# Who subtracts the low parts of the weights in a routed expert kernel: VectorE for GpSimd from the first tile on

## The chip, the cores and the metric

The kernel runs on one core of one Trainium2 chip. A core has five engines that go through their own instructions in order and wait for one another by semaphores: TensorE (PE in the profile) multiplies, VectorE (DVE) and ScalarE (ACT) work on elements, GpSimd (POOL) does so too and issues the DMAs that gather or scatter rows by a list of indices, and SyncE (SP) issues plain DMAs. The metric is the device time of one execution in microseconds; lower is better.

## The reference

A causal mixture over seven earlier positions (a softmax over 7 weights for each of 8 heads) gives 28672 tokens of 192 numbers. A router gives each token to one of 8 experts, by the sorted order of all logits and with room for 3584 tokens in each expert. Each token then goes through its expert's two layers.

```python
logits = x @ w_gate                       # x: 28672 x 192, w_gate: 192 x 8
flat = logits.flatten()
order = np.argsort(-flat)
...
for idx in order:
    tok, e = (int(idx) // E, int(idx) % E)
    if assigned[tok] >= 0 or counts[e] >= cap:
        continue
    assigned[tok] = e
    counts[e] += 1
...
for e in range(E):
    mask = assigned == e
    h = np.maximum(x[mask] @ w1[e], 0.0)  # w1[e]: 192 x 1024
    out[mask] = h @ w2[e]                 # w2[e]: 1024 x 192
```

## The kernel before

**Two stages.** First the mixture is made with Toeplitz matrices on TensorE (`cv`), transposed on VectorE (`aT`), and multiplied with the gate (`pl`, `bg`); the mixed rows go to `attn` in DRAM. This lasts to some 168 us. Then comes the expert stage: 56 tiles of 512 tokens, 7 of each expert. Tile i needs its tokens' rows (`xg`, four gathers by GpSimd, issued two tiles ahead), their transposes and both layers. The loop of `run` goes over tiles i and, within a tile, over eight steps f. A step makes an eighth of layer 1 of tile i (`l1`: five matmuls into a PSUM bank `ph`, of which there are three; ScalarE makes the rounded high part `hh`, VectorE the low part `hl`), a piece of the next tile's preparation (`prep`), half a block of layer 2 of tile i - 1 (`l2`: eight matmuls into `y`), every second step the sum of its halves on VectorE (`yo`) and a scatter to the output on GpSimd.

**High and low parts.** All matrices are split in a rounded high part and the low rest. `wsplit` does this for the weights, piece by piece: ScalarE rounds the raw piece to the high part, then an engine `eng` subtracts it from the raw piece, and SyncE stores both in DRAM for the later tiles of that expert and loads the next raw piece into the buffer that came free (`raw`, four buffers). An expert has eight pieces: `a`, `d`, `a`, `d` (layer 1, rows 0 to 127 and 128 to 191, two halves of the columns each; the low part of a `d` is `dl`) and four of `w` (layer 2). A step of `run` splits at most one piece. The first eight tiles are one of each expert. In tile i the four `w` of its own expert are split in the steps 0 to 3, and the four of layer 1 of the next expert in the steps 4 to 7. With the ninth tile on, weights come back from DRAM, already split. The tests in the last line that the change touches give `d` pieces to VectorE and the others to GpSimd.

**Routing beside the tiles.** Which token belongs to which expert is found out while tiles are running. Five generators make the lists: `half(0)` (512 tokens of each expert, there when the first tile begins), `tail` (the last gate products), `half(1)`, `rest` (rounds of a search for the thresholds, then a list) and `last`. A list is sorted with small matmuls against one-hot tiles that VectorE makes (`oa`). The generators' steps are put between the matmuls when the program is written: `Pace` keeps an account of when each engine will be done (`pe`, `dve`, `act`), and `hook` puts in the next step only while VectorE's account is less than 1.8 us ahead of TensorE's. `Meter` makes the entries, for instructions of TensorE, VectorE and ScalarE. GpSimd has no account: `nc.gpsimd` is the bare engine. Where a result is needed, `drain` runs its generator to the end at once: ahead of tile 1 (`tail`), and in `idx_of` ahead of the first gathers of a list (those of the tiles 8, 24 and 27, issued two tiles earlier).

**Two ways to transpose.** While generators are left, `prep` transposes a tile's rows on TensorE (`px`, one PSUM buffer, emptied by ScalarE and VectorE into `xa` and `xd`). Once they are done (`ff.free`, `free()`), VectorE does it with 16 transposes (`xs`).

Of the kernel before, what the change touches and what calls it, by code (L numbers as in the profile page):

```python
# [1336 lines left out]
def moe_kernel(ctx, tc, x, weight, wg, w1, w2, out):  # L1337
    nc = Pace(tc.nc)
    V, P = nc.vector, nc.gpsimd
# [4 lines left out]
    with ExitStack() as cw:  # L1344
# [11 lines left out]
        ff = FFN(tc, nc, attn, w1, w2, out, r.ident, wr, drm)  # L1356
# [21 lines left out]
        def half(h):  # L1378
            if h == 0:
                yield from r.thresh(0.905)  # L1380
            yield from r.settle(h)
            yield from r.count(r.F, h)
            if h:
                yield from r.counts(NE)
            yield from r.lists(r.F, TA, h, 0 if h else None, *((ia, ja) if h else (ia0, ja0, 8, 4)))

        def rest():
            yield from r.open()
            yield from r.rounds()
            yield from r.final(NL)  # L1390
            yield from r.lists(r.F, TB, 1, None, ib0, jb0, NL, 4)

        def last():
            yield from r.lists(r.F, TB, 0, 1, ib, jb)

        def tail():

            for i in (14, 15):
                for u in range(3):
                    gate(i, u)  # L1400
                    yield PEA if u == 2 else None
                end(i)
            nc.sync.dma_start(r.ltab, LT)
            c1.close()
            cs.close()
            ff.wpool2(cw, 1)
            ff.hp[1] = pool(cw, "fh1", 1, **late)
            yield

        bg = Steps(nc, r, (half(0), tail(), half(1), rest(), last()))  # L1410
# [121 lines left out]
            if i == 1:  # L1532
                bg.drain(3)

        VN = 64
        VP = (1, 3)
        ff.free = set()
        ff.run(idx_of, at, lambda f: P if bg.gens and (ff.done % 8 not in VP or ff.done >= VN) else V, lambda: not bg.gens)
    bi = lst.tile([128, 1], I32, name="bi")
    nc.vector.tensor_copy(bi, r.bad)  # L1540
    bad = nc.values_load(bi[0:1, 0:1], min_val=0, max_val=1)
# [31 lines left out]
```

## Time and profile before

| | |
|---|---|
| median of 3 runs | 1309.41 us (1309.36 to 1313.63) |
| the profiled execution | 1309.36 us, span 1307.3 us |
| TensorE busy | 95% of the span, granted clock 0.982 on average |
| VectorE, ScalarE, GpSimd busy | 77%, 42%, 43% |
| GpSimd's subtractions of weights | 50, of which 48 for `a` and `w` |
| expert stage | from some 168 us to the end |

The busy time of an engine is the time in which one of its instructions ran, waits for data left out. A line such as `L55 DVE ... out<-in xcount | busy, mean | idle before <-releaser` is a group of instructions: L55 is the line of the helper through which nearly all of them are written, so that groups are told apart by the names of their tiles. Numbers of buffers are left out: `X` stands for several scratch tiles of the routing.

### The profile page before, as it was taken

The numbers are of one execution on the slowest core, as the hardware profiler recorded it, in microseconds if no ns is written. First come the engines' busy times: TensorE is split into PE (matmuls) and PEld (weight loads), VectorE is DVE, ScalarE is ACT, GpSimd is POOL, SyncE is SP. The second block draws the span as 40 slices with busy tenths as digits, with TensorE's granted clock in tenths as the row PEclk, the third lists the DMA queues.
The fourth block names the chain that finished last, engine by engine and source line by source line (L and its number), as shares of the span: only waits on it lengthen the run. The fifth ranks groups of instructions, "written<-read, shape, count | busy, mean of one in ns | idle before, by whom it ended". The sixth has DMA issues, their size and how long they took to land.

```text
span 1307.3 us, 21815 instructions
## 1 busy us (share of the span) xinstructions
PE 1247.7 (95%) x7879; PEld 1072.5 (82%) x7879; DVE 1005.3 (77%) x2215; ACT 551.0 (42%) x1214; POOL 556.1 (43%) x549
## 2 busy tenths in 40 slices
PE   5789989988999999999999999999999999999997
PEld 3345568877888988888889999999999999999996
DVE  7488558789998998898757777777777777777772
ACT  5444544574534443443334333333333333333341
POOL 3000457567554344452334444444444444444422
PEclk9999988999999999999999999999999999999999
DMA  9999978579624343342222622332413232131100
GB/s 236 310 292 299 297 260 287 187 260 307 231 96 137 104 148 123 107 148 84 76 90 88 204 97 79 109 102 95 149 41 99 95 102 91 53 135 46 46 25 27
DMA packets 92931, 188.30 MB, mean 144 GB/s; under 512 B 12352, under 2 KB 57872, under 8 KB 88592
## 3 DMA queue, kind: packets, MB, share of 16 engines
q1 hardware_dynamic: 63888, 120.75, 29.4%
q0 software_dynamic: 21504, 44.07, 11.0%
q10 hardware_dynamic: 7424, 22.02, 4.5%
q8 instruction: 63, 1.03, 0.3%
q14 instruction: 52, 0.43, 0.1%
HBM read 114.44 MB, written 72.35 MB: 143 GB/s over the span
## 4 chain that ended last, share of the span: by engine, by line
PE 80%; DVE 9%; DMA 5%; issue 2%; SPq 1%; ACT 1%; POOL 1%; POOLq 0%; DVEq 0%; ACTq 0%
PE ph L55 36%; PE y L55 35%; PE bg L55 3%; DVE X L55 3%; PE cv L55 3%; DMA X<-in_x_dram 3%; DVE hl L55 2%; PE px L55 1%; PE pl L55 1%; DVE aT L55 1%; DMA wgr<-in_moe_w_gate_dram 1%; DMA attn<-a 1%; DMA raw<-in_moe_w_dram 1%; DVE oa L55 1%; SPq L187 0%
## 5 line engine op out<-in xcount | busy, mean ns | idle before, releaser
L55 PE MATMUL y<-w,hh 128*128 128x384 f32 x1792 | 543.0, 358 | 0.0
L55 ACT ACTIVATE hh<-ph 128x512 fp32r<-128x512 f32 x448 | 267.7, 598 | 496.6 <-PE ph L55 472.9
L55 PE MATMUL y<-w,hl 128*128 128x192 f32 x1792 | 450.9, 252 | 0.0
L55 DVE SCALAR_TENSOR_TENSOR hl<-ph,hh 128x512 fp32r<-128x512 f32 x448 | 307.8, 688 | 169.6 <-ACT hh L55 149.2
L55 PE MATMUL ph<-xa,w 128*128 128x512 f32 x1344 | 399.7, 405 | 3.9 <-DVE hl L55 3.9
L55 PEld LDWEIGHTS y<-w,hh 128*128 128x128 f32 x1792 | 339.1, 189 | 22.9 <-issue 6.1
L55 PEld LDWEIGHTS y<-w,hl 128*128 128x128 f32 x1792 | 343.4, 192 | 15.2
L1254 POOL DMA_INDIRECT out_dram<-yo,ib x128 | 128.4, 1003 | 287.7 <-DVE yo L55 277.5
L55 PEld LDWEIGHTS ph<-xa,w 128*128 128x128 f32 x1344 | 221.4, 191 | 24.2 <-DVE hl L55 4.7
L55 DVE STREAM_TRANSPOSE xs<-xg 32x256 f32<-32x256 f32 (+1 forms) x512 | 188.6, 368 | 8.8
L1254 POOL DMA_INDIRECT out_dram<-yo,ia x96 | 105.4, 1098 | 205.0 <-DVE yo L55 169.0
L55 PE MATMUL ph<-xd,w 128*128 128x512 f32 x448 | 179.2, 400 | 1.1 <-DVE xd L55 1.1
L55 PE MATMUL ph<-xd,dl 128*128 128x512 f32 x448 | 175.9, 393 | 1.9 <-DVE dl L55 1.6
L1179 POOL DMA_INDIRECT xg<-attn,jb x128 | 138.2, 1080 | 40.9 <-issue 40.9
L1179 POOL DMA_INDIRECT xg<-attn,ja x96 | 111.8, 1164 | 29.0 <-issue 26.7
L55 PE MATMUL cv<-X,TH 118*128 118x384 f32 x256 | 102.4, 526 | 21.6 <-DVE TH L55 12.5
L55 ACT ACTIVATE yt<-y 128x192 f32<-128x192 f32 x224 | 73.4, 328 | 113.1 <-PE y L55 102.7
L55 DVE TENSOR_TENSOR yo<-y,yt 128x192 f32<-128x192 f32 x224 | 79.5, 355 | 44.0 <-ACT yt L55 40.5
L55 PEld LDWEIGHTS ph<-xd,dl 128*128 128x128 f32 x448 | 85.1, 190 | 22.7 <-DVE dl L55 2.5
L55 PEld LDWEIGHTS ph<-xd,w 128*128 128x128 f32 x448 | 85.1, 190 | 21.2 <-DVE xd L55 1.6
L55 PEld LDWEIGHTS cv<-X,TH 118*128 118x128 f32 x256 | 45.3, 197 | 54.8 <-issue 20.4
L1160 POOL TENSOR_TENSOR w<-raw,w 128x384 fp32r<-128x384 f32 (+1 forms) x48 | 54.1, 1137 | 72.7 <-ACT w L55 37.8
(235 smaller groups left out, 985.7 us busy)
## 6 DMA issues: line engine op xcount, KB each, us to landing
w<-kw SPq DMA_DIRECT2D x16, 1536.0 KB
w<-kv SPq DMA_DIRECT2D x16, 1536.0 KB
X<-in_x_dram SPq DMA_DIRECT2D x16, 1344.0 KB
attn<-a ACTq DMA_DIRECT2D x16, 1344.0 KB
kw<-w SPq DMA_DIRECT2D x48, 256.0 KB
kv<-w SPq DMA_DIRECT2D x32, 384.0 KB
raw<-in_moe_w_dram SPq DMA_DIRECT2D x32, 192.0 KB
raw<-in_moe_w_dram SPq DMA_DIRECT2D x16, 256.0 KB
```

The source lines that it names most:

```text
L55: return f(*a, **k)
L1160: eng.tensor_tensor(lo, r[0:n], hi[0:n].bitcast(F32), op=OP.subtract)
L1179: self.nc.gpsimd.indirect_dma_start(out=t[:, b], out_offset=None, in_=self.attn[0:rows], in_offset=bass.IndirectOffsetOnAxis(ap=idx[b], ax ...
L1254: st = self.nc.gpsimd.indirect_dma_start(out=self.out, out_offset=bass.IndirectOffsetOnAxis(ap=idx, axis=0), in_=o, in_offset=None, bounds ...
```

## The change

One line chooses the engine of the subtraction in the tiles' loop. Now it is VectorE always. The two `a` and two `d` pieces that are split ahead of the first tile stay with GpSimd.

```diff
-        VN = 64
-        VP = (1, 3)
         ff.free = set()
-        ff.run(idx_of, at, lambda f: P if bg.gens and (ff.done % 8 not in VP or ff.done >= VN) else V, lambda: not bg.gens)
+        ff.run(idx_of, at, lambda f: V, lambda: not bg.gens)
```

This moves 46 subtractions, and with them the routing's steps, since VectorE's account now has these entries. What GpSimd's order has from tile 0 to tile 2 before:

```order
L1179 DMA xg<-attn,ja_109 128x192 x4
L1160 TENSOR_TENSOR w_1808<-raw,w_1808 128x2x192 x4
L1160 TENSOR_TENSOR w_1905<-raw,w_1905 128x512 x2
L1179 DMA xg<-attn,ja_109 128x192 x4
L1160 TENSOR_TENSOR w_2039<-raw,w_2039 128x2x192 x3
L1254 DMA out_dram<-yo,ia_105 28672x192
L1160 TENSOR_TENSOR w_2039<-raw,w_2039 128x2x192
L1160 TENSOR_TENSOR w_2226<-raw,w_2226 128x512
```

Four gathers stand ahead of each tile's splits, and scatters between them. The same place now:

```order
L1179 DMA xg<-attn,ja_109 128x192 x8
L1254 DMA out_dram<-yo,ia_105 28672x192 x3
L1179 DMA xg<-attn,ja_109 128x192 x4
L1254 DMA out_dram<-yo,ia_105 28672x192 x4
L1179 DMA xg<-attn,ja_109 128x192 x4
```

Only gathers and scatters are left. On VectorE, the beginning of tile 4 before (`X<-LT,c_T` and what follows with `X` and `c_mu` are the first round of the search):

```order
L55 SCALAR_TENSOR_TENSOR hl<-ph,hh 128x512
L55 SCALAR_TENSOR_TENSOR X_3073<-LT,c_T 128x256 x2
L55 SCALAR_TENSOR_TENSOR hl<-ph,hh 128x512
L55 SCALAR_TENSOR_TENSOR X_3074<-LT,c_T 128x256 x2
L55 TENSOR_TENSOR yo<-y,yt 128x192
L55 SCALAR_TENSOR_TENSOR X_3074<-LT,c_T 128x256 x2
L55 SCALAR_TENSOR_TENSOR hl<-ph,hh 128x512
L55 TENSOR_TENSOR xa<-px,xa 128x512
L55 TENSOR_TENSOR X_3185<-X_3073,X_3074 128x512 x2
```

And now:

```order
L55 SCALAR_TENSOR_TENSOR hl<-ph,hh 128x512
L55 TENSOR_TENSOR w_3091<-raw,w_3091 128x2x192
L55 SCALAR_TENSOR_TENSOR hl<-ph,hh 128x512
L55 TENSOR_TENSOR yo<-y,yt 128x192
L55 TENSOR_TENSOR w_3091<-raw,w_3091 128x2x192
L55 SCALAR_TENSOR_TENSOR hl<-ph,hh 128x512
L55 TENSOR_TENSOR xa<-px,xa 128x512
L55 TENSOR_TENSOR w_3091<-raw,w_3091 128x2x192
```

The splits stand where the round's instructions stood; the round comes later. Counted so, the tiles 4, 5, 6, 7 and 8 have 17, 25, 40, 24 and 33 of VectorE's routing instructions before, and 9, 12, 17, 31 and 30 now. The last generator ends in tile 23, where it ended in tile 22, so that 24 tiles are transposed through `px` instead of 23. On TensorE, the end of tile 0 before (`bg<-aT` are products with the gate, `w_1522` are weights of tile 0, `w_1905` of tile 1):

```order
L55 MATMUL ph<-xa,w_1522 128x512 x3
L55 MATMUL bg<-ident,L 128x128
L55 MATMUL bg<-aT,c_mu 32x128 x24
L55 MATMUL ph<-xd,w_1522 128x512
L55 MATMUL ph<-xd,dl 128x512
L55 MATMUL ph<-xa,w_1522 128x512 x3
L55 MATMUL ph<-xd,w_1522 128x512
L55 MATMUL ph<-xd,dl 128x512
L55 MATMUL ph<-xa,w_1522 128x512 x3
L55 MATMUL bg<-ident,L 128x128
```

And now (`w_1877` are weights of tile 1):

```order
L55 MATMUL ph<-xa,w_1522 128x512 x3
L55 MATMUL ph<-xd,w_1522 128x512
L55 MATMUL ph<-xd,dl 128x512
L55 MATMUL bg<-aT,c_mu 32x128 x24
L55 MATMUL bg<-ident,L 128x128
L55 MATMUL bg<-aT,c_mu 32x128 x24
L55 MATMUL bg<-ident,L 128x128
L55 MATMUL ph<-xa,w_1877 128x512 x3
```

The gate's products are no longer between layer 1's matmuls but behind all of them, put there by the `drain` ahead of tile 1. At the gathers of tile 24 the `drain` in `idx_of` now has four steps to put in, where it had none.

## The prediction

> **What bounds the kernel now.** I read the page's busy shares and slices first, then the time of each tile, then TensorE's own waits, and last the same VectorE instructions inside and outside the stage that the change touches. The page:
>
> ```profile
> span 1307.3 us, 21815 instructions
> PE 1247.7 (95%) x7879; PEld 1072.5 (82%) x7879; DVE 1005.3 (77%) x2215; ACT 551.0 (42%) x1214; POOL 556.1 (43%) x549
> PE   5789989988999999999999999999999999999997
> DVE  7488558789998998898757777777777777777772
> PEclk9999988999999999999999999999999999999999
> ```
>
> TensorE (PE) is busy for 95% of the span, so only time in which it stands or runs at a lower clock can be won back, and what is added to another engine costs nothing until TensorE waits for it. The ninth and tenth slices (some 261 to 327 us) show TensorE at 8 where VectorE (DVE) is at 8 and 9. The change acts in the tiles 0 to 7, from 168 to 360 us. The busy time by tile, a tile beginning at ScalarE's first `hh` of it: rows 1 to 10 are the tiles 0 to 9, row 11 the ten tiles 9 to 18 together, row 12 is tile 24, which has no routing work beside it.
>
> ```profile
> core 0: us, PE busy (x) PEld busy (x) DVE busy (x) ACT busy (x) POOL busy (x), PEclk, DMA share, GB/s
> 167.60:190.50 22.90, 18.87 (x160) 14.00 (x159) 11.22 (x18) 10.40 (x24) 11.78 (x12) 0.85 0.71 238
> 190.50:210.90 20.40, 19.75 (x134) 17.03 (x133) 17.62 (x42) 10.53 (x24) 14.14 (x13) 1.00 1.00 354
> 210.90:247.90 37.00, 34.34 (x277) 30.34 (x277) 26.24 (x58) 14.97 (x28) 21.41 (x17) 0.86 0.55 173
> 247.90:270.00 22.10, 22.01 (x130) 19.70 (x129) 15.09 (x26) 19.02 (x55) 16.42 (x14) 1.00 0.91 292
> 270.00:292.30 22.30, 18.84 (x101) 16.69 (x100) 22.13 (x34) 13.15 (x36) 15.08 (x14) 0.92 0.72 246
> 292.30:311.00 18.70, 18.70 (x110) 16.85 (x110) 18.22 (x45) 12.11 (x27) 15.82 (x14) 1.00 0.92 303
> 311.00:338.80 27.80, 22.51 (x122) 19.75 (x120) 26.84 (x62) 10.84 (x22) 15.80 (x16) 0.88 0.73 237
> 338.80:360.30 21.50, 19.43 (x114) 17.37 (x114) 21.37 (x35) 12.29 (x35) 12.36 (x12) 1.00 0.79 270
> 360.30:381.30 21.00, 20.48 (x122) 18.01 (x121) 19.65 (x57) 6.98 (x15) 10.81 (x11) 1.00 0.34 119
> 381.30:400.50 19.20, 19.20 (x114) 17.37 (x113) 18.48 (x38) 10.77 (x31) 8.40 (x9) 1.00 0.20 55
> 381.30:580.20 198.90, 198.73 (x1174) 177.99 (x1173) 179.50 (x438) 88.43 (x220) 88.18 (x81) 1.00 0.36 119
> 704.60:722.90 18.30, 18.30 (x105) 16.61 (x105) 14.04 (x30) 7.03 (x14) 8.37 (x9) 1.00 0.21 61
> ```
>
> Read the tiles 4, 6 and 7: VectorE is busy for 22.13 of 22.30, 26.84 of 27.80 and 21.37 of 21.50 us, and TensorE is not. These tiles go at VectorE's pace; tile 9, of the same matmuls, takes 19.20 at TensorE's. What TensorE waited for between 225 and 380 us (total, times, longest):
>
> ```profile
> PE bg L55 <- DVE r_cc L55: 5.7, 2, 5.3
> PE px L55 <- issue: 3.5, 1, 3.5
> PE px L55 <- DVE xa L55: 2.1, 1, 2.1
> PE ph L55 <- DVE dl L55: 1.4, 1, 1.4
> ```
>
> All are waits for VectorE: the one named "issue" stands before the transposes `px`, whose only PSUM buffer VectorE had still to empty. The next question is why VectorE is late there. First its groups between 270 and 360 us, then the same groups between 381 and 580 us, where GpSimd makes gathers and scatters only (xcount | busy, mean ns):
>
> ```profile
> L55 DVE SCALAR_TENSOR_TENSOR hl<-ph,hh 128x512 fp32r<-128x512 f32 x31 | 20.9, 678 | 0.0
> L55 DVE SCALAR_TENSOR_TENSOR X<-LT,c_T 128x256 f32<-128x256 f32 x16 | 11.6, 775 | 0.1
> L55 DVE TENSOR_TENSOR dl<-raw,w 64x512 fp32r<-64x512 f32 x7 | 6.5, 924 | 0.0
> L55 DVE TENSOR_TENSOR X<-X,X 128x512 f32<-128x512 f32 x4 | 6.4, 1610 | 0.0
> L55 DVE TENSOR_TENSOR X<-j,r_dd 128x56 f32<-128x56 f32 x2 | 3.0, 1479 | 0.1
> L55 DVE TENSOR_TENSOR r_tl<-T,Ts 128x8 f32<-128x8 f32 x1 | 1.7, 1709 | 0.0
> ...
> L55 DVE SCALAR_TENSOR_TENSOR hl<-ph,hh 128x512 fp32r<-128x512 f32 x80 | 54.6, 684 | 13.1 <-ACT hh L55 9.7 <-issue 3.2
> L55 DVE SCALAR_TENSOR_TENSOR X<-LT,c_T 128x256 f32<-128x256 f32 x48 | 20.0, 480 | 0.2
> L55 DVE TENSOR_TENSOR X<-X,X 128x512 f32<-128x512 f32 x12 | 8.1, 685 | 0.0
> L55 DVE TENSOR_TENSOR X<-j,r_dd 128x120 f32<-128x120 f32 x6 | 1.7, 284 | 0.2
> L55 DVE TENSOR_TENSOR r_tl<-T,Ts 128x8 f32<-128x8 f32 x3 | 0.4, 144 | 0.0
> ```
>
> `hl`, which takes one operand from PSUM, keeps its 0.68 us. Instructions with both operands in SBUF take up to twelve times as long (an 8-column one 1709 ns for 144): they stand still for about as long as a GpSimd subtraction lasts, whose row is
>
> ```profile
> L1160 POOL TENSOR_TENSOR w<-raw,w 128x384 fp32r<-128x384 f32 (+1 forms) x48 | 54.1, 1137 | 72.7 <-ACT w L55 37.8 <-PE cv L55 34.4
> ```
>
> **The change part by part.** *The move.* 46 of these 48 subtractions go to VectorE (two lie ahead of the first tile): 14 of 128x512 and 32 of 128x384. Their price on VectorE has no row. The nearest, from 704 to 887 us, with only gathers and scatters beside them:
>
> ```profile
> L55 DVE TENSOR_TENSOR yo<-y,yt 128x192 f32<-128x192 f32 x41 | 14.7, 358 | 8.8 <-ACT yt L55 8.2
> L55 DVE TENSOR_TENSOR xa<-xs,xa 128x512 fp32r<-128x512 f32 x10 | 6.8, 682 | 0.0
> ```
>
> The wide form is the second row, 0.68 us. 384 columns lie between the ends 0.36 and 0.68; by columns, 0.55, which I take. In all 14 x 0.68 + 32 x 0.55 = 27.1 us (bounds 21.0 and 31.3). The tiles 4 to 7 get 6 wide and 16 narrow ones: 12.9 us.
>
> *The stretch goes.* The quoted groups lose 16 x (775-480) + 7 x (924-682) + 4 x (1610-685) + 2 x (1479-284) + (1709-144) ns = 14.1 us, in the tiles 4 to 7. That more than pays for the 12.9 us.
>
> *The routing work moves later.* The kernel's own pace counts VectorE's splits, never GpSimd's, so it now puts fewer routing steps into these tiles: counted in the order, 99 VectorE routing instructions in the tiles 4 to 8 for 139. One costs (179.50 - 82.5) / 298 = 0.33 us by row 11 (438 instructions, 140 of them the tiles' own: ten times 8 `hl`, 4 `yo`, 2 lows of x at 0.68, 0.35 and 0.68), so 40 x 0.33 = 13.0 us move past tile 8. VectorE's load in the tiles 4 to 8 goes from 108.2 to 108.2 - 14.1 + 12.9 - 13.0 = 94.0 us, 18.8 a tile: near tile 5 and tile 9, which ran 18.22 of 18.70 and 18.48 of 19.20 without holding TensorE.
>
> *What TensorE gets back.* The waits before `px` and for `r_cc` and `xa` are 3.5 + 2.1 + 5.7 = 11.3 us. Behind two of them the granted clock was low: tile 4 loses (1 - 0.92) x 22.3 = 1.8 us; tile 6 loses (1 - 0.88) x 27.8 = 3.3, about 1 of it within the wait. Together 15.4. By the other count, the five tiles took 111.3 us; at 19.2 to 19.9 each (rows 10 and 11) they would take 96.0 to 99.5, so 11.8 to 15.3 less. Small waits will be left where VectorE is at 18.8 of 19.2: I take -14.0.
>
> *Tiles 0 to 3.* VectorE gets 14.2 us there (8 wide, 16 narrow), and is busy for 11.22 of 22.90, 17.62 of 20.40, 26.24 of 37.00 and 15.09 of 22.10, so tile 1 is the tightest, with 3.4 us for 2.8 free; the lead of three PSUM banks covers that. The waits for `dl` (1.4) I leave as they are: -1.4 to +2, taken as 0. GpSimd's four gathers no longer stand ahead of the splits, so the weight buffers come free sooner, but TensorE is fed there: 0.
>
> *A clump at tile 1.* The last gate products and their two transposes, spread over tile 0 before, now stand together ahead of tile 1. Each transpose waits for ScalarE's copy with nothing else to do. Such a wait earlier in the trace:
>
> ```profile
> 162.46 0.33 PE L55 MATMUL pt<-ident,L 128*128 128x128 f32 x1 [0.90 <-ACT L L55]
> ```
>
> Two of them: +1.8 (0 to 2.5).
>
> *The late end.* The third list ends in a drain at tile 22, with TensorE waiting for ScalarE's copy once, as it does today in one place:
>
> ```profile
> L55 PE MATMUL bg<-identb,X 128*128 128x128 bf16 x64 | 5.3, 244 | 1.4 <-ACT X L55 1.4
> ```
>
> So +1.4 (0 to 2.8). The routing work ends a tile later, so tile 24 too is transposed on TensorE: 19.20 - 18.30 = +0.9, while VectorE is rid of that tile's 16 transposes. Gathers and scatters find GpSimd freer; what they feed is two tiles ahead: 0.
>
> **Sum.** The profiled run took 1309.36 us (span 1307.3 and 2.06 around it), within 0.05 of the median 1309.41. 1309.4 - 14.0 + 1.8 + 1.4 + 0.9 = 1299.5. The ends of the terms: -15.4 - 1.4 = 1292.6 at best; -11.8 + 2 + 2.5 + 2.8 + 0.9 = 1305.8 at worst.
>
> **The rivals.** *The gain is given back (1307).* Tiles 1, 2 and 21 to 23 carry the sorts of the lists, where TensorE makes small products and the granted clock was 0.86 in tile 2. Clumped routing work could bring another such stretch at each end: at (1 - 0.86) x 37.0 = 5.2 us for one like tile 2's, and 2 us of waits for a VectorE with 3.4 us more in that tile. For it: tiles 1 and 2 get more VectorE work and no relief as large as in tile 4. Against: tile 2 has 10 us free on VectorE.
>
> *More is won (1291).* The `dl` wait goes too, the clump costs nothing, and one of the low-clock stretches in tile 2 goes as well (2.6 us, half of its 5.2): 1309.4 - 15.4 - 1.4 - 2.6 + 0.9 = 1290.9. For it: the splits of the weights on VectorE are shorter (0.55 to 0.68 for 1.14 us) and wait for no gather.
>
> *VectorE becomes the bound (1326).* If what stretches VectorE is GpSimd's activity as such, the gathers and scatters keep it up, and the tiles 4 to 7 pay the full 12.9 us in stages that VectorE already bounds: 1309.4 + 12.9 + 1.8 + 1.4 + 0.9 = 1326. It decides as soon as less than some 4 us of the 14.1 us of stretch goes and the routing work stays. Against: in tile 24 GpSimd is busy for 8.37 of 18.30 us with gathers and scatters, and `xa<-xs`, both operands in SBUF, still takes 682 ns. The Trainium skill speaks for this rival: Perfetto Trace Analysis, Optimizing Scalar/DVE Operations, says that where VectorE is saturated, handing work to other engines, GpSimd included, may make sense; this change does the reverse in a saturated stage, and by that rule the time would be this rival's. The same section adds that trading work between those two might not help, since they share a read port of SBUF; the stretched rows above are on that second sentence's side.
>
> **How the numbers follow.** A measurement of this kernel tells 0.5%, 6.5 us, from no change. The forecast (1299.5, own range 1294 to 1304) gets 0.60, more won 0.15, gain given back 0.17, VectorE the bound 0.08. Range 1290 to 1308: below it lies a third of "more won" (0.05), above it some 0.07 of "given back" and the last case (0.08), 0.20 in all. Faster than 1302.9: 0.60 x 0.95 + 0.15 + 0.03 = 0.75; slower than 1315.9: 0.08; the rest, 0.17.
>
> **What would show it.** Right: no subtraction on GpSimd after tile 0's start; X<-LT near 480 ns and X<-X,X near 685 everywhere; the tiles 4 to 8 at 19 to 20 us with clock 1.00; `px` and `r_cc` gone from TensorE's waits; two waits for ScalarE's `L` ahead of tile 1; 24 tiles of `px` for 23. Wrong: VectorE busy for all of the tiles 4 to 7 again, groups still stretched beside gathers, or tiles 2 and 21 to 23 longer by more than the tiles 4 to 8 are shorter.

## The result and the profile after

The changed kernel takes 1301.82 us (median of 6 runs, 1297.77 to 1302.96); the kernel before takes 1309.78 us beside it (6 runs). The ratio is 0.9932, interval 0.9914 to 0.9950. Two later comparisons of the same kernel gave 0.9916 (0.9888 to 0.9943) and 0.9924 (0.9904 to 0.9944). Three of the executions behind this document's numbers, one each of E1, E4 and E8, took 1686 to 2363 us and are left out of the ratios. The profiled execution took 1302.88 us. The lines of its page that answer to those of before:

```profile
span 1301.1 us, 21791 instructions
PE 1252.0 (96%) x7887; PEld 1074.6 (83%) x7887; DVE 999.6 (77%) x2245; ACT 550.3 (42%) x1214; POOL 504.1 (39%) x503
PE   6889979999999999999999999999999999999997
DVE  7397558779999989988677777777777777777772
PEclk9899989999999999999899999999999999999999
```

GpSimd has 46 instructions less, and the two slices in which TensorE stood at 8 while VectorE was at 8 and 9 are gone: the ninth and tenth are 9. A new weak place is the sixth slice, where TensorE is at 7. Busy time by stretches of the program, tiles cut as in the prediction: the tiles 0 to 3, then 4, 6 and 7, then the tiles 4 to 8, 9 to 18 and 19 to 23 together and the rest.

```profile
core 0: us, PE busy (x) PEld busy (x) DVE busy (x) ACT busy (x) POOL busy (x), PEclk, DMA share, GB/s
170.50:198.00 27.50, 20.71 (x147) 15.37 (x147) 15.85 (x27) 10.76 (x25) 9.20 (x9) 0.75 0.88 299
198.00:220.90 22.90, 22.90 (x147) 20.26 (x147) 18.55 (x46) 10.82 (x23) 5.05 (x4) 0.93 0.59 199
220.90:252.90 32.00, 31.36 (x278) 28.12 (x278) 22.51 (x46) 14.87 (x28) 16.14 (x12) 0.95 0.72 231
252.90:274.90 22.00, 21.61 (x128) 19.30 (x128) 19.27 (x45) 15.04 (x39) 7.00 (x7) 1.00 0.73 240
274.90:293.80 18.90, 16.95 (x100) 15.17 (x99) 14.60 (x33) 14.89 (x40) 7.95 (x8) 1.00 0.88 299
...
313.50:332.10 18.60, 18.60 (x109) 16.77 (x109) 17.82 (x42) 12.46 (x31) 7.78 (x7) 1.00 0.89 291
332.10:351.90 19.80, 19.80 (x119) 17.73 (x118) 18.63 (x51) 8.38 (x18) 8.47 (x9) 1.00 0.84 287
...
274.90:371.60 96.70, 94.75 (x556) 85.02 (x555) 88.00 (x205) 55.34 (x132) 44.05 (x39) 1.00 0.79 266
371.60:572.40 200.80, 198.99 (x1173) 177.62 (x1172) 181.59 (x449) 89.58 (x225) 89.67 (x81) 1.00 0.36 118
572.40:700.10 127.70, 126.07 (x945) 111.67 (x944) 97.59 (x230) 46.66 (x99) 44.29 (x42) 0.96 0.29 98
700.10:1301.00 600.90, 593.25 (x3387) 539.18 (x3385) 443.64 (x947) 224.78 (x450) 260.06 (x251) 1.00 0.26 88
```

The same stretches of the kernel before, in the tiles 0 and 1, 2 and 3, 4 to 8, 19 to 23 and the rest:

```profile
167.60:210.90 43.30, 38.63 (x292) 31.03 (x291) 28.84 (x59) 20.93 (x47) 25.92 (x24) 0.92 0.85 293
210.90:270.00 59.10, 56.35 (x405) 50.04 (x405) 41.33 (x82) 33.99 (x83) 37.84 (x30) 0.91 0.68 217
270.00:381.30 111.30, 99.96 (x562) 88.68 (x561) 108.21 (x228) 55.36 (x132) 69.86 (x64) 0.95 0.70 234
...
580.20:704.60 124.40, 122.21 (x927) 109.31 (x927) 91.47 (x208) 44.30 (x85) 45.17 (x42) 0.97 0.30 100
704.60:1307.30 602.70, 593.31 (x3387) 539.25 (x3386) 443.62 (x947) 225.41 (x450) 261.05 (x251) 1.00 0.27 87
```

The tiles 4 to 8 went from 111.3 to 96.7 us. VectorE's load there fell from 108.2 to 88.0 us, and the tiles 6 and 7, which were VectorE's, are TensorE's: 18.60 of 18.60 and 19.80 of 19.80 us, at clock 1.00. Against that, the tiles 0 and 1 went from 43.3 to 50.4 us. VectorE's groups in the tiles 4 to 8:

```profile
L55 DVE TENSOR_TENSOR w<-raw,w 128x384 fp32r<-128x384 f32 x16 | 8.8, 548 | 3.8 <-DMA raw<-in_moe_w_dram 3.7
...
L55 DVE SCALAR_TENSOR_TENSOR X<-LT,c_T 128x256 f32<-128x256 f32 x16 | 6.8, 476 | 0.1
...
L55 DVE TENSOR_TENSOR dl<-raw,w 64x512 fp32r<-64x512 f32 x7 | 4.7, 676 | 0.5 <-issue 0.5
L55 DVE TENSOR_TENSOR w<-raw,w 128x512 fp32r<-128x512 f32 x6 | 4.1, 678 | 0.0
...
L55 DVE TENSOR_TENSOR X<-X,X 128x512 f32<-128x512 f32 x4 | 2.6, 680 | 0.0
```

`X<-LT` is back from 775 to 476 ns, `dl` from 924 to 676, `X<-X,X` from 1610 to 680. The moved subtractions have their own rows now, 548 and 678 ns.

What TensorE waits for from tile 0 to tile 9 (total, times, longest):

```profile
PE bg L55 <- issue: 3.0, 4, 1.2
PE ph L55 <- DVE hl L55: 2.6, 1, 2.6
PE px L55 <- DVE xa L55: 2.3, 2, 2.0
PE bg L55 <- ACT L L55: 0.8, 1, 0.8
```

The waits for `r_cc` and `dl` are gone, one `px` wait of 2.0 is left in tile 4. The `bg` waits are new. They are the clump ahead of tile 1, here in order of time on TensorE:

```profile
186.84 0.27 PE L55 MATMUL bg<-aT,c_mu 128*32 128x128 f32 x1 [0.45 <-issue]
188.25 0.38 PE L55 MATMUL bg<-aT,c_mu 128*32 128x128 f32 x2 [1.15 <-issue]
189.79 0.90 PE L55 MATMUL bg<-aT,c_mu 128*32 128x128 f32 x22 [1.16 <-issue]
191.49 0.48 PE L55 MATMUL bg<-ident,L 128*128 128x128 f32 x1 [0.80 <-ACT L L55]
191.89 2.79 PE L55 MATMUL bg<-aT,c_mu 128*32 128x128 f32 x48
195.23 0.48 PE L55 MATMUL bg<-ident,L 128*128 128x128 f32 x1 [0.55 <-DMA kd<-dl]
```

The two transposes wait 0.80 and 0.55 us; the profile puts the second down to a DMA here, and to ScalarE's `L`, again with 0.55, in the next profiled execution. The products with the gate before them stop three times, 2.76 us in all, for nothing that the profile shows. Behind the clump the granted clock is half:

```profile
192.00:201.00 9.00, 8.45 (x65) 7.16 (x66) 3.66 (x8) 1.99 (x6) 0.00 (x0) 0.50 0.83 314
```

The 0.75 over tile 0 also holds a low stretch at its start, 0.71 from 170.5 to 182 us, which the kernel before has too (0.76 from 167.6 to 182). From there to the end of tile 1 the kernel before ran at 1.00.

### The profile page after: what moved, and what is told of

Read it like the earlier page. It is cut to its first block, busy times and chain, and to the rows that moved or that the text cites. A ratio compares the mean times of both kernels' runs of the same rounds, so it can differ in the third digit from the quotient of the medians.

```text
span 1301.1 us, 21791 instructions
## 1 busy us (share of the span) xinstructions
PE 1252.0 (96%) x7887; PEld 1074.6 (83%) x7887; DVE 999.6 (77%) x2245; ACT 550.3 (42%) x1214; POOL 504.1 (39%) x503
## 4 chain that ended last, share of the span: by engine, by line
PE 83%; DMA 8%; DVE 4%; ACT 2%; issue 1%; SPq 1%; POOL 1%; another core or an unknown queue 0%; POOLq 0%; DVEq 0%; ACTq 0%
PE ph L55 39%; PE y L55 37%; DMA X<-in_x_dram 5%; PE bg L55 3%; PE cv L55 2%; PE px L55 1%; DMA attn<-a 1%; DVE hl L55 1%; DVE X L55 1%; DMA wgr<-in_moe_w_gate_dram 1%; DMA raw<-in_moe_w_dram 1%; PE pl L55 1%; DVE oa L55 1%; SPq L187 0%; DMA kd<-dl 0%
## 5 line engine op out<-in xcount | busy, mean ns | idle before, releaser
L1254 POOL DMA_INDIRECT out_dram<-yo,ib x128 | 127.7, 998 | 288.5 <-DVE yo L55 278.3
L55 DVE STREAM_TRANSPOSE xs<-xg 32x256 f32<-32x256 f32 x496 | 182.9, 369 | 8.5
L55 PE MATMUL cv<-X,TH 118*128 118x384 f32 x256 | 105.9, 542 | 21.7 <-DVE TH L55 12.4
L55 DVE TENSOR_TENSOR yo<-y,yt 128x192 f32<-128x192 f32 x224 | 79.5, 355 | 46.5 <-ACT yt L55 42.7
L55 ACT ACTIVATE a<-cv 128x384 f32<-128x384 f32 x128 | 61.5, 490 | 57.7 <-PE cv L55 48.2
```

The lines of the kernel that those rows point to most:

```text
L55: return f(*a, **k)
L1254: st = self.nc.gpsimd.indirect_dma_start(out=self.out, out_offset=bass.IndirectOffsetOnAxis(ap=idx, axis=0), in_=o, in_offset=None, bounds ...
```

## The experiments

The experiments ran on three chips, E1 to E3 on one, E4 to E6 on the second, E7 and E8 on the third, each beside the kernel before, whose median was 1310.85, 1314.62 and 1314.64 us there. So ratios can be compared throughout, times only on one chip.

**The question.** Two things came with the one line: another engine subtracts, and the pace's account of VectorE gets an entry for each subtraction, so that routing steps come later. The theory behind the prediction's sum was that the two work together: the stretch that goes (14.1 us) pays for the subtractions (12.9 us), and the later steps (13.0 us) are the gain. Its rivals: the stretch alone is the gain, or the pace alone is, and the engine doesn't matter.

**E1: only the account.** GpSimd keeps every subtraction; each is entered in VectorE's account as if VectorE had made it, so TensorE's order is that of the changed kernel.

```diff
+class Charged:
+    def tensor_tensor(self, lo, a, b, op):
+        p = self.nc
+        p.dve = max(p.dve, p.pe) + max(0.08 + max(map(size, (lo, a, b))) / 960, 0.18)
+        return self.eng.tensor_tensor(lo, a, b, op=op)
...
+        C = Charged(nc, P)
-        ff.run(idx_of, at, lambda f: P if bg.gens and (ff.done % 8 not in VP or ff.done >= VN) else V, lambda: not bg.gens)
+        ff.run(idx_of, at, lambda f: C if bg.gens and (ff.done % 8 not in VP or ff.done >= VN) else V, lambda: not bg.gens)
```

> GpSimd keeps the subtractions, but the pace enters each of them into VectorE's account, so the routing steps stand as in the changed kernel and GpSimd's order as in the kernel before. If the stretched VectorE instructions are half of the gain: they stay stretched (X<-LT,c_T near 775 ns), the tiles 4 to 8 take some 103 us (111 before, 97 after), time some 1307 us. If the later routing work alone made the gain: tiles 4 to 8 near 97 us, time 1302 us like the changed kernel.

Ratio 0.9997 (0.9981 to 1.0013). The time is near that of the first case, but its reason does not hold: the tiles 4 to 8 gained all that the changed kernel gains there. Below, the tiles 0 and 1, the tiles 4 to 8, a stretched group in the latter, and TensorE's clump ahead of tile 1:

```profile
168.50:224.50 56.00, 41.73 (x293) 34.69 (x293) 30.09 (x59) 21.76 (x48) 25.73 (x25) 0.82 0.68 231
285.70:382.50 96.80, 94.88 (x556) 85.07 (x555) 85.85 (x183) 54.93 (x132) 69.36 (x64) 1.00 0.79 268
```

```profile
L55 DVE SCALAR_TENSOR_TENSOR X<-LT,c_T 128x256 f32<-128x256 f32 x16 | 10.1, 682 | 0.1
```

```profile
184.80 1.06 PE L55 MATMUL bg<-aT,c_mu 128*32 128x128 f32 x32
192.88 0.47 PE L55 MATMUL bg<-ident,L 128*128 128x128 f32 x1 [7.02 <-ACT L L55]
193.28 2.79 PE L55 MATMUL bg<-aT,c_mu 128*32 128x128 f32 x48
198.90 0.47 PE L55 MATMUL bg<-ident,L 128*128 128x128 f32 x1 [2.83 <-DMA kd<-dl]
```

VectorE is still stretched (682 ns for 476), and it doesn't matter, since it is busy for 85.85 of 96.80 us. The tiles 0 and 1 give the gain back: 56.0 us for 43.3. The transpose waits 7.02 us for ScalarE's `L`, and ScalarE has in the same time

```profile
185.50 0.63 ACT L55 ACTIVATE w<-raw 128x512 fp32r<-128x512 f32 x1 [4.54 <-DMA raw<-in_moe_w_dram]
...
192.41 0.21 ACT L55 ACTIVATE L<-bg 128x64 f32<-128x64 f32 x1
```

The copy stands in ScalarE's order behind roundings of the weights that wait for the next raw piece. So the clump has a price that depends on who is queued ahead of the copy.

**E2: only the engine.** VectorE subtracts, through the bare engine, so that no entry is made and TensorE's order is that of before.

```diff
+        R = tc.nc.vector
-        ff.run(idx_of, at, lambda f: P if bg.gens and (ff.done % 8 not in VP or ff.done >= VN) else V, lambda: not bg.gens)
+        ff.run(idx_of, at, lambda f: R if bg.gens and (ff.done % 8 not in VP or ff.done >= VN) else V, lambda: not bg.gens)
```

> VectorE makes the subtractions, but they are not entered in its account, so the routing steps stand where the kernel before has them, with no clump at tile 1 and no late end. If the freed stretch is what counts: X<-LT,c_T at 480 ns, VectorE's load in the tiles 4 to 8 is 108 - 14 + 13 = 107 us, these tiles take 100 to 104 us, the tiles 0, 1 and 19 to 23 are as before, time some 1300 us. If only the later routing work counts: VectorE's added 13 us lengthen the tiles 4 to 7, time 1310 us or more.

Ratio 0.9942 (0.9926 to 0.9958). The tiles 4 to 8, and TensorE's waits in them:

```profile
275.80:381.00 105.20, 97.86 (x564) 85.80 (x563) 102.22 (x249) 54.98 (x132) 47.85 (x41) 1.00 0.75 248
```

```profile
PE bg L55 <- DVE r_cc L55: 4.4, 3, 2.8
PE px L55 <- DVE xa L55: 2.0, 2, 1.3
```

105.2 us for 111.3, a little more than expected: without the stretch, but with all the old routing steps, VectorE is busy for 102.22 of them, and the waits for `r_cc` and `px` remain. Apart from the subtractions E2 has VectorE's instructions of the kernel before, so it also sizes the whole stretch there: from tile 4's first `hl` to tile 9's, these instructions lasted 16.9 us less in E2, summed one by one.

**E3: tile 0 as before.** From the changed kernel; GpSimd keeps tile 0's subtractions, without an entry, so that tile 0's gate products stay spread.

```diff
-        ff.run(idx_of, at, lambda f: V, lambda: not bg.gens)
+        ff.run(idx_of, at, lambda f: P if ff.done < 12 and ff.done % 8 not in (1, 3) else V, lambda: not bg.gens)
```

> The changed kernel with the eight splits of tile 0 as before, so that the gate's products stand between layer 1's matmuls again; tiles from 4 on as in the changed kernel. If the clump ahead of tile 1 cost what the tiles 0 and 1 lost (27.5 and 23.0 us for 22.9 and 20.4): 5 to 7 us less than the changed kernel, some 1296 us, no low clock around 191 us. If that loss was chance of one execution or the splits on VectorE themselves: some 1302 us.

Ratio 0.9891 (0.9865 to 0.9917). In the profiled execution, the shortest of six (1290.39 us, median 1295.52), the tiles 0 and 1 took 45.1 us, the tiles 4 to 8 as follows:

```profile
268.80:364.10 95.30, 93.89 (x549) 84.19 (x548) 87.68 (x203) 56.18 (x135) 45.16 (x38) 1.00 0.79 267
```

The changed kernel itself, beside these three:

> The changed kernel again, for comparison on the same chip: 1298 to 1303 us.

Ratio 0.9916 (0.9888 to 0.9943), with 47.4 us in the tiles 0 and 1 and 96.6 in the tiles 4 to 8. A third profiled execution, beside E7 and E8, took 99.6 in the tiles 4 to 8, with a wait of 3.2 for `px` in tile 4.

**E4: GpSimd busy again.** From the changed kernel. Beside each of the 46 moved subtractions GpSimd subtracts a scratch tile from itself, which nobody waits for; the order and the account are the changed kernel's.

```diff
+class Beside:
+    def tensor_tensor(self, lo, a, b, op):
+        s = self.scratch[:, 0:size(lo)]
+        self.nc.gpsimd.tensor_tensor(s, s, s, op=OP.subtract)
+        return self.nc.vector.tensor_tensor(lo, a, b, op=op)
...
+        B = Beside(nc, extra)
-        ff.run(idx_of, at, lambda f: V, lambda: not bg.gens)
+        ff.run(idx_of, at, lambda f: V if ff.done % 8 in (1, 3) else B, lambda: not bg.gens)
```

> The changed kernel, and beside each of the 46 moved subtractions GpSimd subtracts a scratch tile of the same size from itself; nothing waits for that. It gives back the stretch alone. If the stretch costs little once fewer routing steps stand in these tiles: X<-LT,c_T is stretched again in part, some 9 us in the tiles 4 to 8, and these take 97 to 100 us; time 1299 to 1303 us. If the stretch is what made the kernel before slow: 106 us or more in these tiles, time 1309 us or more.

Ratio 0.9993 (0.9974 to 1.0012): the whole gain is gone, more than was expected. The tiles 4 to 8, VectorE's subtractions from tile 0 on, and the largest of TensorE's waits:

```profile
277.90:378.50 100.60, 96.03 (x558) 85.29 (x557) 92.74 (x205) 55.68 (x131) 69.09 (x62) 1.00 0.78 261
```

```profile
L55 DVE TENSOR_TENSOR w<-raw,w 128x384 fp32r<-128x384 f32 x32 | 20.2, 630 | 3.8 <-DMA raw<-in_moe_w_dram 3.7
```

```profile
PE px L55 <- DVE xa L55: 5.4, 4, 2.6
PE bg L55 <- ACT L L55: 5.2, 1, 5.2
```

The stretch comes back in part. In the tiles 4 to 8 VectorE is busy for 92.74 us instead of 88.00 with the same instructions: 4.7 us, far less than the kernel before loses. The narrow subtractions take 630 ns for 548; `X<-LT`, which was expected to be stretched, keeps its 476, since no extra subtraction ran beside one. TensorE waits for VectorE before `px` again, and the tiles 4 to 8 take 1.0 to 4.0 us more than in the three executions of the changed kernel (96.7, 96.6 and 99.6). The 5.2 us are the clump's: as in E1, ScalarE's copy of `L` stands behind a rounding of the weights, which starts late, at 189.05 us, after 2.27 us in which it waits for nothing that the profile shows. The tiles 9 to 23 took 5 us more than in the changed kernel's execution beside E3, on another chip; but on E4's own chip the other three profiled executions took 330.0 to 330.7 us there, and E4 332.6. So E4 shows that GpSimd's load at the changed kernel's order takes the gain away, and not how much of this the tiles 4 to 8, the clump and the clock have each.

**E5: the account again, from tile 1 on.** E1 without its clump: before, with entries for GpSimd's subtractions only once tile 0 is done. No subtraction changes its engine.

```diff
-        ff.run(idx_of, at, lambda f: P if bg.gens and (ff.done % 8 not in VP or ff.done >= VN) else V, lambda: not bg.gens)
+        ff.run(idx_of, at, lambda f: (C if ff.done >= 12 else P) if bg.gens and (ff.done % 8 not in VP or ff.done >= VN) else V, lambda: not bg.gens)
```

> GpSimd keeps all its subtractions, but from tile 1 on the pace enters them into VectorE's account; tile 0 is not entered, so that nothing is clumped ahead of tile 1. No instruction changes its engine. If the later routing steps make the gain and the clump took it back in the run with all entered: tiles 0 and 1 some 44 us, 2 and 3 some 60, 4 to 8 some 97; time some 1299 us. If the engine of the subtractions decides: 1308 us or more.

Ratio 0.9894 (0.9866 to 0.9922). The tiles 4 to 8, and TensorE's only wait in them:

```profile
279.30:374.60 95.30, 93.89 (x549) 84.12 (x548) 83.28 (x181) 56.40 (x135) 67.08 (x61) 1.00 0.78 265
```

```profile
PE px L55 <- DVE xa L55: 1.4, 1, 1.4
```

This is E3's 95.3 us, and TensorE's order is E3's, but GpSimd subtracts (67.08 us busy for 45.16). The profiled execution as a whole was the longest of E5's six (1309.02 us, median 1301.46), by times outside these tiles. E3 once more, beside it:

> The changed kernel with tile 0 split as before, again, for comparison on the same chip: 1291 to 1300 us.

Ratio 0.9891 (0.9867 to 0.9915). So at this order on TensorE it makes no difference that can be measured who subtracts; the intervals would hide some 0.4%. It does at the other two orders: E2 has TensorE's order of the kernel before and is 0.6% faster, and the changed kernel has E1's and is 0.7% faster.

**E6: is it tile 0's order, or GpSimd?** E3, with the same order on TensorE, but VectorE subtracts in tile 0 too, without an entry.

```diff
-        ff.run(idx_of, at, lambda f: V, lambda: not bg.gens)
+        ff.run(idx_of, at, lambda f: R if ff.done < 12 and ff.done % 8 not in (1, 3) else V, lambda: not bg.gens)
```

> The changed kernel, but the splits of tile 0 on VectorE are not entered in its account, so that the gate's products stand between the matmuls as before and GpSimd still makes no subtraction. If the clump alone is the loss in tile 0: as with tile 0 on GpSimd, 1295 us. If GpSimd's gathers ahead of the splits also held tile 1: 1 to 3 us less. If VectorE's splits in tile 0 cost something themselves: 1299 us.

Ratio 0.9911 (0.9883 to 0.9938), between E3 and the changed kernel, and its interval takes in both: inconclusive. The profiled execution had 46.6 us in the tiles 0 and 1, and 95.4 in the tiles 4 to 8.

**E7 and E8: where must the entries be?** E5 with entries in the tiles 4 to 7 only (E7), and in the tiles 1 to 3 only (E8).

```diff
-... (C if ff.done >= 12 else P) ...
+... (C if ff.done >= 36 else P) ...
-... (C if ff.done >= 12 else P) ...
+... (C if 12 <= ff.done < 36 else P) ...
```

> GpSimd keeps its subtractions; the pace enters them into VectorE's account only in the tiles 4 to 7. 104 of VectorE's routing instructions stand in the tiles 4 to 8 (139 before). If the account must hold what VectorE loses where VectorE is the bound: tiles 0 to 3 as before, some 102 us, tiles 4 to 8 some 97 to 99 us, ratio to the kernel before 0.989 to 0.993. If later steps in the tiles 1 to 3 made the gain: 0.998 or more.

> The counterpart: entered in the tiles 1 to 3 only, 121 routing instructions in the tiles 4 to 8. If the account must hold in the stage itself: the stretch of some 15 us meets full tiles again, tiles 4 to 8 take 104 to 110 us, ratio 0.996 to 1.002. If it is enough that the steps come later: tiles 4 to 8 some 97 us, ratio 0.990.

E7: 0.9920 (0.9895 to 0.9945). E8: 0.9986 (0.9962 to 1.0009). The tiles 4 to 8 of E7 and of E8, and E8's longest wait in them:

```profile
272.20:370.70 98.50, 96.15 (x553) 86.35 (x553) 91.88 (x191) 53.99 (x132) 70.37 (x64) 0.98 0.78 264
```

```profile
266.40:371.20 104.80, 97.49 (x553) 86.53 (x552) 94.84 (x202) 59.73 (x151) 69.02 (x62) 0.97 0.73 241
```

```profile
PE bg L55 <- DVE r_cc L55: 3.9, 1, 3.9
```

Counted in the order, VectorE has 99 routing instructions in the tiles 4 to 8 in E5 and in the changed kernel, 104 in E7, 121 in E8, 139 before and in E2. E8 puts them back into the stage that VectorE bounds, and a long wait for `r_cc` is back (E7 has one of 1.8). In the profiled executions this is not all of E8's loss: its tiles 4 to 8 are still shorter than the 111.3 us before, but its tiles 9 to 18 took 206.6 us, with a wait of 3.4 for `r_v`, where all others took 199 to 203. The changed kernel beside these two:

> The changed kernel once more, for comparison on the same chip: ratio to the kernel before 0.991 to 0.994.

Ratio 0.9924 (0.9904 to 0.9944).

**Together.** Ratios to the kernel before:

| | no entry | entries from tile 0 | entries from tile 1 |
|---|---|---|---|
| GpSimd subtracts | 1 (before) | 0.9997 (E1) | 0.9894 (E5) |
| VectorE subtracts | 0.9942 (E2) | 0.9932, 0.9916, 0.9924 (the change) | 0.9911 (E6); 0.9891 twice with tile 0 on GpSimd (E3) |

Each of the two alone makes the kernel faster, and they don't add up, for both give VectorE room in the same tiles, where TensorE won 16 us at most (95.3 for 111.3). The first rival (the stretch alone) holds for half of the best gain, 0.6% of 1.1%; the second (the pace alone) for all of it, if the clump is avoided. The best kernels are E3 and E5. They beat the kernel before by 1.1%; beside the changed kernel their intervals touch its own (0.9891 and 0.9894 for 0.9916 to 0.9932).

## Why the prediction was right, and where it was not

The time was forecast as 1299.5 and is 1301.82 us. By the steps, from the windows above and the starts of tile 0 (167.6 and 170.5), in the profiled executions:

| step | forecast | measured |
|---|---|---|
| tiles 4 to 8 | -14.0 | 111.3 to 96.7: -14.6 |
| clump, tiles 0 and 1 | +1.8 | 43.3 to 50.4: +7.1 |
| tiles 2 and 3 | 0 | 59.1 to 54.0: -5.1 |
| tiles 9 to 18 | 0 | 198.9 to 200.8: +1.9 |
| late end and one more `px`, tiles 19 to 23 | +2.3 | 124.4 to 127.7: +3.3 |
| before tile 0; after tile 23 | 0; 0 | +2.9; -1.8 |
| sum | -9.9 | -6.3 (span -6.2) |

That the time was met within 2.3 us is partly luck: the clump cost 5.3 us more than forecast, and the tiles 2 and 3 gave 5.1 us for which nothing had been put down. Small slips in the working move nothing: tile 1's splits come to 3.6 us by their prices, not 3.4; the best end leaves out the 0.9 for tile 24; and a 56-column row of the stretch is compared with a 120-column one.

**The main term is right, by its reason too.** The tiles 4 to 8 gave 14.6 us for 14.0 (14.7 and 11.7 in the other two executions). The moved subtractions cost 16 x 548 + 6 x 678 ns = 12.8 us there (12.9 forecast), the stretch is gone, and routing steps moved. VectorE's load fell further than forecast, to 88.0 us for 94.0, because both of its parts were larger: summed instruction by instruction, the stretch was 16.9 us for the 14.1 of the groups in the sum, and the 40 steps lasted 14.7 us in E2, for 13.0. So stretch and subtractions do not nearly cancel, as in the sum; the move alone takes VectorE from 108.2 to 102.2 us (E2). But once the steps are gone, that no longer matters: E5 against E3.

**"VectorE becomes the bound" is refuted.** Gathers and scatters do not stretch VectorE: `X<-LT` is at 476 ns beside 44 us of them. The Trainium skill, SBUF — State Buffer, Who interferes with whom, says that a VectorE instruction with two SBUF inputs contends with a GpSimd instruction that reads SBUF; the rows agree, 476 ns in the changed kernel, 682 in E1 beside GpSimd's subtractions. And of what the Trainium skill says in Perfetto Trace Analysis, Optimizing Scalar/DVE Operations, the second sentence, that work traded between these two might not help, is borne out at one order (E5 0.9894, E3 0.9891); at the order of the kernel before, taking the subtractions off GpSimd did help (E2 0.9942).

**The clump was mis-sized.** Its two waits are as forecast (0.80 and 0.55 us for 0.90 each), but that was not its whole price. In the profiled execution the clock accounts for 5.1 us of the 7.1: (1 - 0.83) x 50.4 = 8.6 us lost for (1 - 0.92) x 43.3 = 3.5, 0.83 being the mean over both tiles. The pauses at the gate products (2.76) and the two waits (1.35), less a wait for `hl` that was 1.2 shorter than before, are roughly the rest. The low clock comes with the clump: some 9 us behind it ran at 0.50 here, at 0.82 and 0.88 in the other two executions of the changed kernel, at 0.50 in E1 and 0.52 in E4, while the same place was at 1.00 in all eight profiled executions without a clump. The clump's price varies: the tiles 0 and 1 of the changed kernel took 50.4, 47.4 and 44.9 us in three profiled executions, part of that by a wait for `hl` in tile 0 (2.65, 4.65, 1.83) that comes with or without the clump. Less that wait it is 47.8, 42.7 and 43.1, a mean of 44.5, for 40.8 in the eight profiled executions without a clump, each less its longest such wait: +3.7 us. E3's ratio of 0.9891 for the changed kernel's mean of 0.9924 says 4.3, but their intervals overlap, and E6 (0.9911), which has no clump either, is between them. What the term left out is the clock behind the clump and the pauses; the row it was priced by, a transpose with an idle ScalarE, held for the two waits, and E1 shows what else can be queued ahead of the copy. During the pauses "issue" ScalarE stands too (2.89 us before its next `hh`, for which VectorE then waits); what they are stays open.

**Tiles 2 and 3 gained, where 0 was said.** The clock gives most: (1 - 0.97) x 54.0 = 1.6 us lost for (1 - 0.91) x 59.1 = 5.3. That is the last piece of "more is won", which named one low-clock stretch in tile 2. In all three executions of the changed kernel these tiles took 53.3 to 54.7 us. In E2, E3 (twice) and E6, where VectorE subtracts there too and tile 0 has no clump, they took 56.0 to 56.9, so about half of the gain comes without the clump; but E8, where GpSimd subtracts, took 55.7. How the clump changes tile 2 wasn't tried.

**The late end** came at 3.3 for 2.3, but not as priced: the wait of 1.4 for ScalarE's copy is gone, and E3, with the same steps there, took 123.6 us at clock 0.99, while E6 took 130.0 at 0.93. The clock in the sorts moves this term by more than the change does. The end after tile 23 is 1.8 us shorter; in the profiled executions in which GpSimd subtracts beyond tile 0 it lasts 601.4 to 602.7, in the others 600.6 to 601.0. Why isn't known.

## What to carry to other kernels

Where a program's order is set by an account of when engines will be done, an account that leaves out time in which an engine is blocked fills the very stage that this engine bounds; enter the blocked time and try that alone before moving work between engines. Price a moved instruction together with what it does to the order, and then with what stands ahead of it in each in-order queue: a 0.2 us copy behind a rounding that waits for a load held TensorE for 7 us. When two remedies free the same engine in the same stage, their gains do not add.

## What the chip showed beyond this

A stretched instruction lasts until the subtraction beside it is over, whatever its own size: in the kernel before, the 8-column one of 144 ns took 1709, to 317.59 us, and GpSimd's subtraction ended at 317.55. The mean of a group hides this. Of the 16 `X<-LT` in the tiles 4 to 7, three took 1.7 to 2.6 us, the longest beside two subtractions in a row, and 13 kept some 480 ns. GpSimd's indirect DMAs do nothing of the kind: in the changed kernel 33 of the 64 `X<-LT` ran while GpSimd issued one, and took 477 ns, and the other 31 took 478. The granted clock is a large source of difference between executions of the same instructions: the tiles 19 to 23 took 123.6 us at 0.99 and 127.6 at 0.96 in two profiled executions of E3, which ran on two chips.
